# Opening attention on the first 512 rows and running all feed-forward work inside the first 16 attention blocks

## The chip, the core and the metric

The kernel runs on one core of a Trainium2 chip. A core has five engines that run independently and meet through semaphores: TensorE (PE, matmul), VectorE (DVE), ScalarE (ACT), GpSimd (POOL) and SyncE (SP, which here only issues DMAs). Each engine takes its instructions strictly in the order in which the program gave them: an instruction that waits holds up all behind it on that engine. TensorE writes its results to eight PSUM banks of 512 float32 columns; six of them form the ring `ps_r` (three slots of two banks), two are the accumulator `ps_acc` of the attention's values.

The metric is the device time of one execution in microseconds.

## The reference

```
x  = A_x                                  # [1, 2048, 512]
xn = (x - mean(x)) / sqrt(var(x) + 1e-5)  # per row
q  = (xn @ wq) as 32 heads of 128
p  = softmax(q @ k_cache^T / sqrt(128))   # 2048 keys per head
s  = concat_heads(p @ v_cache) @ wo       # back to 512 columns
gate, up = xn @ W_gate, xn @ W_up         # 512 -> 1792
h  = gate * (gate > 0) * up
g  = silu(h @ W_down)                     # 1792 -> 512
out = x + s * g
```

All inputs are bfloat16.

## The kernel before

Rows are taken in four quarters Q of 512. Attention is cut into 128 blocks, one for each head and quarter (head outermost); a block has 8 pairs of 128-key tiles. For a pair, `emit_S_tile` (L1567) computes scores into one ring slot by two matmuls of 512 columns, ScalarE takes their exponential into `PT` (L1579), and `emit_PV_tile` (L1676) multiplies by the values in eight matmuls of 129 columns; the 129th column collects the softmax sum. Scores run three pairs ahead of the values (`LAG`). At the end of a block VectorE takes the reciprocal of the sums and writes the normalised block (`emit_norm_block`, L1596 and L1599), and a DMA on SP turns it (L1604). The value product of the next block waits for that normalisation, since it writes the same banks.

Everything else is placed between these pairs. The main loop (L1964) goes through the pairs in order: scores, then the work that the table `plan` holds for this pair (`emit_M`), then smaller work of `side`, then values. The order on each engine is thus the order in which this loop emits.

Many products are done by seven products in place of eight: two halves of the rows, two halves of the contraction and two halves of the columns are combined by sums beforehand and by VectorE additions afterwards. `emit_st` does so for the query projections of two heads (L914), `emit_gu` for gate and up (L1167), `emit_d` for down (L1228), `emit_unit` and the functions after it for later query and output projections.

What matters around the change:

- Start: x is loaded, normalised and turned; quarter 0 goes through gate, up and down with plain products (`head_ln`, `emit_gate_up(0)`, `emit_down`), before any attention. Then quarter 2 goes through gate and up with plain products (`emit_gate_up(2)`), into whose end the first query projections and scores are woven. Row statistics use VectorE (L419, L424, L436, L439) and a square root on ScalarE (L431); the table of ScalarE's functions is switched from the square root to tanh and exp by an `ACT_TABLE_LOAD`.
- Quarters 1 and 3 go through gate and up as one pair by seven products (`emit_gu`), two products per pair of attention, in pairs 1 to 5 of the blocks 2 to 12. The slab weights come through SP (`gu_load`), are scaled on ScalarE (L626) and combined on POOL (`gu_sums`, L636 to L641).
- Down is done by seven products for quarters 2, 1 and 3 (`emit_d`).
- Query projections of the first eight heads are done by `emit_st`, from weight sums that POOL makes (`emit_sw`, L659 to L672).
- `emit_tx`, `emit_wd_scale`, `emit_wd_sums` and `emit_hs` make the sums that the products by seven need from the rows, the down weights and the hidden values.

From block 16 on nothing of the feed-forward part is left until its result is multiplied in at the end.

Of the kernel before, what the change touches and what calls it, by code (L numbers as in the profile page):

```python
# [5 lines left out]
BF16 = mybir.dt.bfloat16  # L6
# [46 lines left out]
def bass_recurrent_scan__mha_block_cached__glu_gated_reglu__prompt_kernel(  # L53
# [63 lines left out]
    with ExitStack() as es:  # L117
# [9 lines left out]
        def newsem(unit=1):  # L127
# [16 lines left out]
        Wq_sb = [S_([128, DC, 2, Dh], BF16, "Wq_sb") for _ in range(2)]  # L144
        Wo_sb = [S_([128, G, D], BF16, "Wo_sb") for _ in range(2)]
# [4 lines left out]
            "p (i c s) -> p i c s", i=4, c=DC // 2)  # L150
# [8 lines left out]
        o_h, o_wd, o_x = 0, 28672, 43008  # L159
        hT0 = at_(o_h, [128, FC, NQ], BF16, "hT0")  # L160
        hT = [at_(o_h + 14336 * i, [128, FC, NQ], F16, "hT") for i in range(2)]
        Wd_sb = at_(o_wd, [128, FC, D], BF16, "Wd_sb")
        Wd16 = at_(o_wd, [128, FC, D], F16, "Wd16")
        x_sb = at_(o_x, [128, NT, D], BF16, "x_sb")
        WdT = at_(o_x, [128, 3, HF, D // 2], F16, "WdT")
        HS_sb = at_(53760, [128, 3, HF, NQ // 2], F16, "HS_sb")
        xc_sb = at_(59392, [128, 4, D], BF16, "xc_sb")
        xcT = at_(63488, [128, DC, NQ], BF16, "xcT")
        Wg_sb = at_(67584, [128, DC, F], BF16, "Wg_sb")
        Wu_sb = at_(81920, [128, DC, F], BF16, "Wu_sb")  # L170
        gr_sb = [at_(96256 + 1024 * i, [128, NQ], BF16, "gr_sb") for i in range(NSLOT)]
        sig_sb = [at_(99328 + 2048 * i, [128, D], F32, "sig_sb") for i in range(2)]
        small = [103424]

        def sm_(shape, dt, name):
            t = at_(small[0], shape, dt, name)
            small[0] += (4 * shape[1] * (shape[2] if len(shape) > 2 else 1) + 31) // 32 * 32
            assert small[0] <= 104448
            return t

        r2 = sm_([128, 4, 1], F32, "r2")
        r2h = sm_([128, 4, 1], F32, "r2h")
# [4 lines left out]
        nmr = sm_([128, NT, 1], F32, "nmr")  # L187
        rz_sb = sm_([128, 4, 1], F32, "rz_sb")
# [3 lines left out]
        cuv0 = [at_(10240 - 2048 * i, [128, NQ], F32, "cuv0") for i in range(2)]  # L192
        SW0 = at_(12288, [128, 4, DC // 2, Dh], F16, "SW0")
        cuv = [at_(92160 + 2048 * i, [128, NQ], F32, "cuv") for i in range(2)]
        o_w2, o_sg = (64512, 99328, 96256), (104448, 106496, 101376)
# [3 lines left out]
        gcu = [at_(53760 + 2048 * i, [128, NQ], F32, "gcu") for i in range(2)]  # L199
        gcv = at_(57856, [128, NQ], F32, "gcv")  # L200
        uA = [at_(59904 + 1024 * i, [128, NQ], BF16, "uA") for i in range(2)]
        uB = [at_(61952 + 1024 * i, [128, NQ], BF16, "uB") for i in range(2)]
        gA = [at_(o, [128, NQ], BF16, "gA") for o in (66560, 98304)]
        gB = at_(108544, [128, NQ], BF16, "gB")
        dbuf = {Q: [at_(o, [128, 2, D // 2], F32, "dbuf") for o in os_] for Q, os_ in (
            (2, tuple(range(0, 12288, 2048))), (1, o_w2 + o_sg))}
        dbuf[3] = dbuf[1]
# [20 lines left out]
        sem_wg = [newsem(16) for _ in range(4)]  # L228
        sem_wu = [newsem(16) for _ in range(4)]
# [44 lines left out]
        sem_ln3 = newsem()  # L274
        sem_ln4 = newsem()
# [4 lines left out]
        sem_h = newsem()  # L280
        sem_g = newsem()
        sem_qpe = newsem()
        sem_da = newsem()
# [5 lines left out]
        sem_sq = newsem()  # L289
        sem_relu = newsem()  # L290
        sem_sig = newsem()
        sem_exp = newsem()
        sem_tp = newsem()
        sem_gate = newsem()
        sem_gu = newsem()
        sem_y = newsem()
# [17 lines left out]
        FCS = [0, 2, 5, 9, FC]  # L314
        HFC = 2
        wg_src = B_W_gate.rearrange("(c p) f -> p c f", p=128)
        wu_src = B_W_up.rearrange("(c p) f -> p c f", p=128)

        def load_w(eng, dst, src, sems, k):
            a, b_ = FCS[k] * 128, FCS[k + 1] * 128  # L320
            if b_ > a:
                sems[k].sig(eng.dma_start(dst[:, :, a:b_], src[:, :, a:b_]))
# [1753 lines left out]
```

## Time and profile before

| what | value |
|---|---|
| median of 3 runs | 1240.26 us (1240.01 to 1240.39) |
| profiled execution, span from first to last instruction | 1238.8 us |
| instructions in it | 29098 |
| mean granted TensorE clock | 0.999 |

The profile is of one execution, and gives no time of its own for it beside the span; the median of the runs lies 1.5 us above the span. A page of the profile lists the busy time of each engine, then the chain of work that ended last, then groups of instructions by line. A group's row reads: line, engine, operation, tile written <- tiles read, shapes, count | busy time in us, mean ns of one | idle time of the engine before them and what ended it. In the view by stages a row reads: window, length, then the busy time and count of each engine in it, the granted clock, the DMA share and GB/s.

### The profile page before, as it was taken

Reading aid. Unit: us, or ns where it says so; the run is one execution under the profiler, and the core shown is the slowest. Engines: PE = TensorE matmul, PEld = TensorE weight load, DVE = VectorE, ACT = ScalarE, POOL = GpSimd, SP = SyncE. Lnnn points to the kernel's source line nnn. Section 1 sums busy time; section 2 is a strip of 40 time slices with the busy share of each in tenths; the row PEclk is TensorE's granted clock in tenths of the full one; section 3 lists DMA queues with packets and bytes.
Section 4 is the critical chain, followed back from the end, with each engine's and each line's share of the span. In section 5 each row is a group of like instructions: output and inputs, shape, how many; then the busy total and the mean of one; then the engine's idle time right before and its main releaser. Section 6 shows DMA issues by size and latency. Waiting matters only on the chain.

```text
span 1238.8 us, 29098 instructions
## 1 busy us (share of the span) xinstructions
PE 1233.0 (100%) x11937; PEld 817.5 (66%) x11937; DVE 874.2 (71%) x1313; ACT 1040.0 (84%) x1109; POOL 730.2 (59%) x840
## 2 busy tenths in 40 slices
PE   9999999999999999999999999999999999999998
PEld 5466666776666666666666666666666666666665
DVE  7668787667676767676776777676776677675587
ACT  3457877668888998989989999989999989989994
POOL 3355876313757557655866565846775576662368
PEclk9999999999999999999999999999999999999999
DMA  9712331323222333233122332234222322238626
GB/s 276 158 31 37 76 81 24 52 48 96 53 50 52 65 70 52 48 69 60 41 35 52 74 61 51 50 69 69 49 52 50 46 56 48 52 69 129 124 35 141
DMA packets 279012, 85.25 MB, mean 69 GB/s; under 512 B 253024, under 2 KB 278880, under 8 KB 278880
## 3 DMA queue, kind: packets, MB, share of 16 engines
q1 hardware_dynamic: 277536, 82.61, 34.5%
q8 instruction: 95, 1.56, 0.6%
q10 hardware_dynamic: 1344, 0.79, 0.2%
q14 instruction: 37, 0.30, 0.1%
HBM read 36.96 MB, written 4.19 MB: 33 GB/s over the span
## 4 chain that ended last, share of the span: by engine, by line
PE 98%; DVE 1%; DMA 0%; ACT 0%; issue 0%; SPq 0%; DVEq 0%
PE ps_acc L1676 37%; PE ps_r L1567 36%; PE ps_r L1050 5%; PE ps_r L1167 3%; PE ps_r L1406 3%; PE ps_r L1228 3%; PE ps_r L1466 2%; PE ps_r L914 2%; PE ps_r L729 2%; PE ps_r L733 2%; PE ps_acc L832 1%; PE ps_r L1708 1%; PE ps_r L1497 1%; PE ps_r L1498 0%; DMA x_sb<-in_A_x_dram 0%; PE ps_r L1789 0%
## 5 line engine op out<-in xcount | busy, mean ns | idle before, releaser
L1579 ACT ACTIVATE PT<-ps_r 128x1024 bf16<-128x1024 f32 x1024 | 988.6, 1025 | 129.7 <-PE ps_r L1567 117.6
L1676 PEld LDWEIGHTS ps_acc<-V_sb,PT 128*128 128x128 bf16 x8192 | 545.3, 98 | 231.0 <-issue 29.5
L1676 PE MATMUL ps_acc<-V_sb,PT 128*128 128x129 bf16 x8192 | 632.4, 220 | 0.0
L1567 PE MATMUL ps_r<-QT_sb,KT_sb 128*128 128x512 bf16 x2048 | 605.1, 379 | 0.2 <-DVE s_acc L1386 0.2
L1055 DVE TENSOR_TENSOR UVR<-UVR,ps_r 128x512 f32<-128x512 f32 (+1 forms) x228 | 168.6, 755 | 85.3 <-PE ps_r L1050 83.1
L1376 DVE TENSOR_TENSOR s_acc<-s_acc,ps_r 128x1024 f32<-128x1024 f32 x130 | 156.7, 1218 | 32.7 <-PE ps_r L1406 22.5
L1567 PEld LDWEIGHTS ps_r<-QT_sb,KT_sb 128*128 128x128 bf16 x2048 | 161.2, 98 | 26.4 <-DVE UVR L1055 4.3
L1015 POOL TENSOR_TENSOR TI<-xn_sb 128x512 f16<-128x512 f16 x48 | 55.8, 1162 | 97.0 <-PE ps_r L1050 97.0
L1384 DVE TENSOR_TENSOR s_acc<-s_acc,ps_r 128x512 f32<-128x512 f32 x116 | 77.4, 685 | 22.1 <-PE ps_r L1466 17.9
L1599 DVE TENSOR_TENSOR Onorm<-ps_acc,rz_sb 128x512 bf16<-128x512 f32 x127 | 87.8, 691 | 4.4
L1055 DVE TENSOR_TENSOR QT_sb<-UVR,ps_r 128x512 bf16<-128x512 f32 x72 | 49.5, 687 | 52.9 <-PE ps_r L1050 50.5
L1596 DVE RECIPROCAL rz_sb<-ps_acc 128x4 f32<-128x4 f32 x127 | 23.0, 181 | 82.3 <-PE ps_acc L1676 81.7
L1434 POOL TENSOR_TENSOR TI<-OX 128x512 f16<-128x512 f16 x28 | 31.7, 1155 | 65.1 <-issue 65.1
L1015 POOL TENSOR_TENSOR TI<-xnT 128x512 f16<-128x512 bf16 x36 | 41.5, 1154 | 39.7 <-PE ps_r L1050 21.4
L1322 POOL TENSOR_TENSOR WX<-Wo_sb 128x512 f16<-128x512 bf16 x7 | 8.1, 1156 | 90.4 <-DVE Wo_sb L1312 51.3
L1015 POOL TENSOR_TENSOR TI<-xn_sb,TI 128x512 f16<-128x512 f16 x48 | 55.8, 1163 | 0.0
L1123 POOL TENSOR_TENSOR QT_sb<-UVR,UVR 128x512 bf16<-128x512 f32 x24 | 29.8, 1271 | 39.9 <-DVE UVR L1055 39.9
L1050 PE MATMUL ps_r<-TI,SI 128*128 128x512 f16 x126 | 47.8, 379 | 0.0
L1123 POOL TENSOR_TENSOR UVR<-UVR,UVR 128x512 f32<-128x512 f32 x24 | 29.8, 1272 | 25.0 <-DVE UVR L1055 25.0
L1015 POOL TENSOR_TENSOR TI<-xnT,TI 128x512 f16<-128x512 bf16 x36 | 41.6, 1156 | 0.0
L1143 POOL TENSOR_SCALAR gB<-gB 128x512 bf16<-128x512 bf16 x14 | 20.8, 1484 | 30.3 <-DVE gB L1173 30.3
L1434 POOL TENSOR_TENSOR TI<-OT_store 128x512 f16<-128x512 bf16 (+1 forms) x28 | 32.0, 1163 | 9.3 <-issue 8.6
(232 smaller groups left out, 1357.2 us busy)
## 6 DMA issues: line engine op xcount, KB each, us to landing
V_sb<-in_A_v_cache_dram SPq DMA_DIRECT2D x32, 512.0 KB, 4.2
Wq_sb<-in_A_wq_dram SPq DMA_DIRECT2D x16, 256.0 KB, 3.2
Wo_sb<-in_A_wo_dram SPq DMA_DIRECT2D x8, 512.0 KB, 4.6
out_dram<-g_sb SPq DMA_DIRECT2D x4, 512.0 KB, 5.1
OT_store<-Onorm SPq DMA_TRANSPOSE x127, 2.5
Wd_sb<-in_B_W_down_dram SPq DMA_DIRECT2D x1, 1792.0 KB, 14.2
W<-in_B_W_gate_dram SPq DMA_DIRECT2D x14, 128.0 KB, 2.4
W<-in_B_W_up_dram SPq DMA_DIRECT2D x14, 128.0 KB, 3.0
```

The costliest lines, as they stand in the source:

```text
L1015: return sem_ui.sig(pool.tensor_tensor(dst, x, y, o))
L1050: return sem_up.sig(pe.matmul(dst, lhs, rhs, start=start, stop=stop, skip_group_check=True))
L1055: dve.tensor_tensor(dst, x, ps, ALU.add))
L1123: u_tok["add"] = u_tok[("add", i)] = sem_uv.sig(pool.tensor_tensor(dst, UU[:, i, :], RR[:, i, :], ALU.add))
L1167: ins = pe.matmul(ps_r[:, bank, :], L(i), R(i), start=(i == 0), stop=(i == HC - 1))
L1376: t = sem_opa.sig(dve.tensor_tensor(dst, dst, sb, op))
L1384: t = dve.tensor_tensor(dst, dst, sb, op)
L1434: return sem_oi.sig(pool.tensor_tensor(dst, x, y, o))
L1567: ins = pe.matmul(ps_r[:, 2 * s + tt, :], KT_sb[h % 2][:, t * 128:(t + 1) * 128], QT_sb[qt_slot[(h, Q)]][:], start=True, stop=True)
L1579: act.activation(PT[pb][:], ps_r[:, 2 * s:2 * s + 2, :], ACTF.Exp, scale=scale / WSC)
L1599: dve.tensor_tensor(Onorm[ob][:], o_ap, rz_sb[:].to_broadcast([128, 4, Dh]), ALU.mult))
L1676: ins = pe.matmul(o_ap, PT[pb][:, tt, j * 128:(j + 1) * 128], V_sb[vb][:, t, 0:VW], start=(t == 0 and j % 2 == 0), stop=(t == KT - 1 and j ...
```

## The change

Order of the work. The first 512 rows are normalised, turned on TensorE, and at once projected to the queries of heads 0 to 3 by plain products (`front`). Attention opens then. The blocks of heads 0 and 1 alternate for the first eight blocks (`hq_of`), so that the quarters 1 to 3 are needed later; their queries for heads 0 and 1, and quarter 2 for heads 2 and 3, come from plain products in the loop (`emit_qplain`). The other rows' coefficients use a reciprocal square root by Newton steps on VectorE in place of ScalarE's square root.

```diff
+        def front():
+            c0 = head_first_transpose(head_norm(0))
+            warm_mm(3)
+            nt = {n: head_norm(n) for n in range(1, 4)}
+            act.activation(warm_sb[:], eps_sb[:], ACTF.Tanh)
+            slots = [ring_acquire() for _ in range(HQ // 2)]
...
+            _wait(pe, c0[0])
+            head_q(0, al, range(0, DC // 2))
+            _wait(pe, c0[1])
+            head_q(0, al, range(DC // 2, DC))
+            c1 = head_transpose(1, nt[1])
+            _wait(pe, c1)
+            head_q(1, lo, cc)
+            c2 = head_transpose(2, nt[2])
+            head_q(1, hi, cc)
+            c3 = head_transpose(3, nt[3])
+            _wait(pe, c2)
+            head_q(2, al, cc)
+            _wait(pe, c3)
+            p = head_q(3, al, cc)
+            toks = {0: q_out(act, 0, 0, ps_r[:, 0, :], p[0])}
+            stok = [ln_stats(4), ln_stats(5)][-1]
+            toks[1] = q_out(dve, 1, 0, ps_r[:, 1, :], p[1])
+            ring_tok[0] = [toks[0], toks[1]]
+            stok = [ln_stats(6), ln_stats(7)][-1]
+            for h in (2, 3):
+                toks[h] = q_out(dve, h, 0, ps_r[:, h, :], p[h])
+            ring_tok[1] = [toks[2], toks[3]]
+            ctok = ln_coef(list(range(4, 8)), stok)
+            ln_rows_norm(1, ctok)
+            ln_rows_turn(1)
+            for Q in (2, 3):
+                ctok = ln_rows(Q)
+                if Q == 3:
+                    gu_prep(0, pool)
+                ln_rows_norm(Q, ctok)
+                if Q == 2:
+                    ln_rows_turn(2)
+            gu_prep(1, pool)
...
+            op(dve.tensor_scalar(v, mv[:, a:b_, 1:2], 1e-5, None, op0=ALU.add))
+            op(dve.tensor_scalar(t.bitcast(I32), v.bitcast(I32), 1, None, op0=ALU.logical_shift_right))
+            tok = op(dve.tensor_scalar(y.bitcast(I32), t.bitcast(I32), -1.0, float(0x5f3759df), op0=ALU.mult, op1=ALU.add))
+            for _i in range(3):
+                op(dve.tensor_tensor(t, y, y, ALU.mult))
+                op(dve.scalar_tensor_tensor(t, t, -0.5, v, op0=ALU.mult, op1=ALU.mult))
+                tok = op(dve.scalar_tensor_tensor(y, t, 1.5, y, op0=ALU.add, op1=ALU.mult))
...
+        def hq_of(b):
+            if b < 2 * QB:
+                return b % 2, b // 2
+            return divmod(b, QB)
```

Here `head_norm` normalises one row tile (coefficients, then the scaling on VectorE for tile 0 and on POOL for the others), `head_q` gives the short query matmuls of a row tile, and `op` waits for its own result before the next.

Feed-forward. All four quarters go through gate and up by seven products, as the row pairs (0, 2) and (1, 3): 28 slabs, two products in each pair of attention, in a cycle of seven steps for two slabs. One ring slot is held for the whole of it, and the products of a slab are added up in its banks: a product may start when the bank's last partial sum has been read. Down follows by seven products for all four quarters, in the order 2, 0, 3, 1.

```diff
+        gu_cycle = (((0, 1, 0), (0, 6, 1)), ((0, 2, 0), (0, 5, 1)), ((0, 3, 1), (0, 7, 0)),
+                    ((1, 1, 1), (0, 4, 0)), ((1, 2, 1), (1, 6, 0)), ((1, 5, 0), (1, 7, 1)),
+                    ((1, 3, 0), (1, 4, 1)))
+        gu_steps = [[(c + o, m, k) for o, m, k in st] for c in range(0, NCH, 2) for st in gu_cycle]
...
+            if m == 1:
+                _wait_all(pe, [t[(c, "s")], t.get((c - 1, "gB"))])
+                if k == 0:
+                    _wait_all(pe, xt_ready[pair] + xt_ready[pair + QB // 2])
+            elif m == 6:
+                _wait_all(pe, [t[(c, "x")], t.get((c - 1, "uA"))])
+                if k == 0:
+                    _wait(pe, tx_tok[(pair, 3)])
+            else:
+                _wait(pe, t[(c, {2: "c1", 5: "c6", 3: "c65", 7: "gA", 4: "uB"}[m])])
...
+        def gu_hi(c):
+            pair, k = divmod(c, FC)
+            _wait_all(dve, [gu_tok[(c, "gB")], gu_tok[(c, "uB")]])
+            if pair and k == 0:
+                _wait(dve, (sem_dp, 7))
+            h_done[(pair + QB // 2, k)] = sem_gud.sig(
+                dve.scalar_tensor_tensor(hT[1][:, k, :], gB[:], 0.0, uB[:], op0=ALU.max, op1=ALU.mult))
...
+        def emit_gu(n):
+            if not gu_slot:
+                gu_slot.append(ring_acquire(hold=True))
+            s = gu_slot[0]
+            st = gu_steps[n]
+            for c, m, k in st:
+                p = gu_prod(c, m, 2 * s + k)
+                gu_out(c, m, 2 * s + k, p)
+                if m == 3:
+                    hi_c = c
+            if any(m == 3 for _, m, _k in st):
+                gu_hi(hi_c)
+            for c, m, k in st:
+                if m == 4 and c + NW < NCH:
+                    gu_load(c + NW)
+                    gu_later.append((n + 4, c + NW))
+            if gu_later and n >= gu_later[0][0]:
+                gu_prep(gu_later.pop(0)[1])
```

`gu_out` reads a partial sum: product 2 by ScalarE (ReLU), the others by VectorE; after product 4 POOL multiplies the lower quarter's hidden values, and `gu_hi` does the upper quarter's on VectorE. `gu_prep` scales a slab on ScalarE and makes its four sums on POOL (slabs 0 and 1 on POOL alone).

The places, in pairs P counted from the first (block P // 8, pair P % 8):

```diff
+        GU0, GU1 = 13, 67
...
+        for n in range(len(gu_steps)):
+            half = len(gu_steps) // 2
+            put(GU0 + n if n < half else GU1 + n - half, (emit_gu, 0, n))
+        for P, h, Q in ((8, 0, 1), (10, 1, 1), (20, 0, 2), (24, 1, 2), (30, 0, 3), (34, 1, 3), (38, 2, 2), (42, 3, 2)):
+            put(P, (emit_qplain, 1, h, Q))
+        for P, pr, c, step in ((46, 1, 1, 0), (50, 1, 1, 1), (54, 1, 1, 2), (61, 1, 1, 3),
+                               (76, 2, 0, 0), (82, 2, 0, 1), (88, 2, 0, 2), (94, 2, 0, 3),
+                               (98, 2, 1, 0), (104, 2, 1, 1), (108, 2, 1, 2), (113, 2, 1, 3)):
+            put(P, (emit_st, 1 if step == 3 else 2, pr, c, step))
+        for Q, ps in ((2, (63, 64, 65, 66)), (0, (68, 69, 70, 71)),
+                      (3, (117, 118, 119, 120)), (1, (122, 123, 124, 125))):
+            for k, P in enumerate(ps):
+                put(P, (emit_d, 1 if k == 3 else 2, Q, k))
+        for Q, ps in ((2, (53, 54, 55, 56, 62, 62, 62, 63)), (0, (66, 66, 67, 67, 67, 68, 68, 68)),
+                      (3, (106, 107, 108, 109, 115, 116, 116, 117)), (1, (120, 120, 120, 121, 121, 121, 122, 122))):
+            for k, P in enumerate(ps):
+                aside(P, emit_hs, Q, k // 4, k % 4)
+        aside(8, ln_rows_turn, 3)
+        for k in range(4):
+            aside(10 + k // 2, emit_tx, 0, k)
+            aside(17 + k, emit_tx, 1, k)
+            aside(30 + 6 * k, emit_wd_sums, k)
+        aside(20, load_wd)
+        aside(25, emit_wd_scale, 0)
+        aside(28, emit_wd_scale, 1)
+        aside(36, lambda: (_wait(sp, qp_done_tok[0]), issue_wq(2)))
+        aside(43, emit_sw, 1)
+        aside(68, emit_sw, 2)
...
+            if (bq, pq) == (12, 4):
+                emit_sw(3)
```

The loads of keys, values and query weights of the first heads move to the very start, on SP and ACT; the keys of head 2 are loaded at the start of block 7, one block ahead.

781 lines of the change are left out of this document (277 added, 504 removed).

## The prediction

> **What bounds the kernel now.** I read the page first: the span, the busy shares and the chain that ended last.
>
> ```profile
> span 1238.8 us, 29098 instructions
> PE 1233.0 (100%) x11937; PEld 817.5 (66%) x11937; DVE 874.2 (71%) x1313; ACT 1040.0 (84%) x1109; POOL 730.2 (59%) x840
> PE 98%; DVE 1%; DMA 0%; ACT 0%; issue 0%; SPq 0%; DVEq 0%
> ```
>
> The page warns that a matmul's end is modelled, so I also took the view of who waited for whom, for PE (us, times, longest). First and last of its four rows:
>
> ```profile
> PE ps_r L475 <- PEq L2061: 0.8, 1, 0.8
> ...
> PE ps_r L1567 <- DVE s_acc L1386: 0.2, 1, 0.2
> ```
>
> The largest is 0.8 us, and that lies before the first matmul: TensorE waits next to nothing in the whole span. It is the bound everywhere, so the change pays by matmul time that it takes away, and costs by every microsecond for which TensorE has nothing it may start. That ScalarE's exponentials begin earlier is worth nothing. True paces come from the chain in order of time (start, us, what):
>
> ```profile
> 9.08 1.79 PE ps_r L541 x32
> 31.59 12.09 PE ps_acc L832 x56
> 74.51 3.06 PE ps_r L1228 x28
> 312.94 0.91 PE ps_acc L1676 x16
> ```
>
> A matmul costs 0.056 us at 128 columns, 0.216 at 512, 0.109 at 256, and 0.057 in the attention's value product. One pair of attention is 2 x 0.216 + 8 x 0.057 = 0.89 us.
>
> **Matmul work.** Stage view, whole span, restricted in turn to lines 729, 733, 832, 1167, 914 and 1228; count in brackets:
>
> ```profile
> 0.00:1238.80 1238.80, 26.69 (x104) 10.06 (x104) 1.00 0.35 69
> 0.00:1238.80 1238.80, 26.69 (x104) 10.17 (x104) 1.00 0.35 69
> 0.00:1238.80 1238.80, 12.25 (x56) 5.49 (x56) 1.00 0.35 69
> 0.00:1238.80 1238.80, 50.46 (x196) 19.13 (x196) 1.00 0.35 69
> 0.00:1238.80 1238.80, 29.42 (x112) 10.78 (x112) 1.00 0.35 69
> 0.00:1238.80 1238.80, 34.08 (x294) 28.52 (x294) 1.00 0.35 69
> ```
>
> Of 512 columns 208 + 56 + 196 + 112 = 572 go. They are replaced by 28 slabs x 7 products x 2 = 392 for gate and up, 8 x 4 = 32 in emit_qplain, and 14 + 28 + 28 = 70 in emit_st: 494. Down grows from 294 to 4 x 98 = 392 of 256 columns. The 64 short gate/up matmuls of the head become 64 short query matmuls. Net: -78 x 0.216 + 98 x 0.109 = **-6.1 us**. From the seventeenth block on, the instructions are those of before: 0.
>
> **The front.** Rows of the timeline (start, us):
>
> ```profile
> 3.49 0.69 DVE L419 BATCH_NORM_STATS2 stats<-x_sb 128x6 f32<-128x512 bf16 x1 [3.49 <-DMA x_sb<-in_A_x_dram]
> 9.12 0.58 ACT L467 COPY xcT<-ps_acc 128x512 bf16<-128x512 bf16 x1 [0.62 <-PE ps_acc L462]
> 10.70 1.03 PE L729 MATMUL ps_acc<-xcT,Wg_sb 128*128 128x512 bf16 x4
> 14.53 0.16 DVE L436 RECIPROCAL rstd<-sqv 128x4 f32<-128x4 f32 x1
> 14.72 0.16 DVE L439 SCALAR_TENSOR_TENSOR nmr<-mv,rstd 128x4 f32<-128x4 f32 x1
> 16.52 0.38 DVE L424 BATCH_NORM_AGGREGATE mv<-stats 128x2 f32<-128x6 f32 x4
> 31.37 1.28 ACT L840 ACT_TABLE_LOAD   x1
> 206.19 0.69 DVE L1173 TENSOR_TENSOR gcu<-gcu,ps_r 128x512 f32<-128x512 f32 x1 [0.21 <-PE ps_r L1167]
> 206.79 0.68 DVE L1173 TENSOR_TENSOR uB<-gcv,ps_r 128x512 bf16<-128x512 f32 x1
> ```
>
> By 10.70 us the old kernel has run 80 short matmuls (4.5 us): 6.2 us lost, then nothing. In the new one a row tile costs VectorE statistics 0.69, aggregate 0.2, a root on ScalarE 0.2 with two hand-overs, reciprocal 0.16: about 1.35 us, so the fourth root ends near 9.2. ScalarE then loads the tanh table (1.28), and the copies of tiles 1 to 3 are queued behind it: the first ends near 11.3. Copies, transposes and 48 short matmuls alternate until about 14.5; the first scores start near 14.7. VectorE takes three head outputs and two statistics from 14.2 to 17.3 (0.6 us from one operation to the next), then three coefficient chains: 4 aggregates 0.38 and 12 dependent small operations at 0.19, 2.8 us; the second and third with 4 statistics, 5.3 us each. It is free at **30.7**. The first block's normalisation is queued behind them (0.9 us), and the ninth value product waits for that: 31.6. TensorE, in order, has by then run 80 short matmuls, 12 score pairs, 8 value pairs and one emit_qplain: 4.5 + 5.2 + 3.6 + 0.9 = 14.2 us. Lost 17.4 against 6.2: +11.2. Then four emit_tx (0.6 to 0.69 each) stand between VectorE's next query output and the first slab's product 6: +0.9. **Front +12.1.** Bounds: if the dependent small operations ran at the aggregates' 0.1, 36 x 0.09 = 3.3 less; and never under 14.7 - 4.5 - 6.2 = +4.0, the first score's own delay.
>
> [...]
>
> ```profile
> 0.76 3.92 PE L475 MATMUL ps_r<-const-bfloat16-1.0 128*128 128x256 bf16 x18 [0.76 <-PEq L2061]
> ```
>
> Those 18 run at 0.22 us where 256 columns cost 0.109 later, so a slow start is seen; a fall back is not, TensorE never idling so long. [...]
>
> **Queues and loads.**
>
> ```profile
> KT_sb<-in_A_k_cache_dram SPq DMA_TRANSPOSE x32, 4.2
> W<-in_B_W_up_dram SPq DMA_DIRECT2D x14, 128.0 KB, 3.0
> L1579 ACT ACTIVATE PT<-ps_r 128x1024 bf16<-128x1024 f32 x1024 | 988.6, 1025 | 129.7 <-PE ps_r L1567 117.6
> L626 ACT ACTIVATE W<-W 128x1024 bf16<-128x1024 bf16 x14 | 14.7, 1052 | 1.4 <-DMA W<-in_B_W_up_dram 1.4
> ```
>
> The third head's keys, moved on SP to one block ahead, have 8 pairs (14 us) for 4.2. A slab has four pairs (7 us) for 3.0 plus issue; SP has issued its loads by the time the rows 4 to 15 are there to be turned, and the block's own transposes stand behind those turns; nothing of it is asked for before VectorE's 30.7. ScalarE per pair: 1.03, and per seven pairs two 0.6 copies and two scales: 1.5 of 1.75 us. I cost these at 0; without the cover a late slab holds ScalarE, and the exponentials with it, by its lateness.
>
> **The gate/up stretch** (98 pairs). A pair becomes 0.43 scores, 0.86 two products, 0.46 values: 1.75 us. Products now add up in a bank, so each waits on PE for VectorE's (twice in seven pairs ScalarE's) reading of the one before; scores and values stand behind it. From the pair's start, first product done 0.86, VectorE 0.2 later (row of the 0.69 read above: after its product, 0.2), done 1.75, needed 2.18; second read done 2.4, needed 2.61. Little over 0.2 us is spare.
>
> ```profile
> L1599 DVE TENSOR_TENSOR Onorm<-ps_acc,rz_sb 128x512 bf16<-128x512 f32 x127 | 87.8, 691 | 4.4
> L1596 DVE RECIPROCAL rz_sb<-ps_acc 128x4 f32<-128x4 f32 x127 | 23.0, 181 | 82.3 <-PE ps_acc L1676 81.7
> L1250 DVE SCALAR_TENSOR_TENSOR g_sb<-dbuf,dbuf 128x512 bf16<-128x512 f32 x12 | 10.1, 848 | 0.3
> L768 DVE TENSOR_SCALAR Wd_sb<-Wd_sb 128x3584 bf16<-128x3584 bf16 x2 | 2.8, 1416 | 0.0
> ```
>
> *Block ends.* Old plans leave pairs 6 and 7 of a block without products; now VectorE's normalisation (0.18 + 0.69) queues behind this pair's reads and the next value product needs it at 3.04. After two reads it ends at 3.4 (0.4 late), after one 0.15 late, after three (gu_hi, not in the trace, 0.69 to the 0.85 of the nearest row; I take 0.7) 1.0 late. Of twelve ends in the stretch four, three and five are of three, one and two reads: 4.0 + 0.45 + 2.0 = **+6.5**.
>
> *Bursts.* Single extra operations (emit_tx, a query output) fit the room or come with their own matmuls. Around pairs 53 to 56 and 106 to 109, though, three pairs bring VectorE 13 operations at 0.64 (8.3 us; the first also a normalisation) against 3 x 1.75 + 0.86 = 6.1 of TensorE: about 2 us late each. emit_wd_scale (1.4) twice, less the room: 0.5 each. **+5.** Both terms lie between 0 (reads overlap more) and twice that (VectorE holds 0.9 of the stretch, one lateness feeding the next).
>
> *POOL.*
>
> ```profile
> L659 POOL TENSOR_SCALAR Wq_sb<-Wq_sb 128x1024 bf16<-128x1024 bf16 x2 | 5.5, 2774 | 6.4 <-DMA Wq_sb<-in_A_wq_dram 6.4
> L636 POOL TENSOR_TENSOR SG<-W 128x256 f16<-128x256 bf16 x14 | 9.3, 667 | 17.4 <-ACT PT L1579 13.3 <-ACT W L626 4.1
> L445 POOL TENSOR_SCALAR xn_sb<-x_sb,rstd,nmr 128x512 bf16<-128x512 bf16 x16 | 12.1, 768 | 21.1 <-DVE nmr L439 21.1
> L1145 POOL TENSOR_TENSOR hT<-gA,uA 128x512 f16<-128x512 bf16 x14 | 16.5, 1180 | 1.2 <-DVE uA L1173 1.1
> L779 POOL TENSOR_TENSOR WdT<-Wd_sb 128x1792 f16<-128x1792 bf16 x1 | 3.6, 3569 | 0.0
> ```
>
> In the front POOL normalises rows 4 to 7 from 20.1, rows 8 to 11 from 25.4 (3.1 us each), then gu_prep(0), 2.8 + 4 x 0.67 = 5.5, until 34.0, rows 12 to 15 until 37.1 and gu_prep(1) until 42.6; product 6 of the two slabs asks at about 36.5 and 45: 0, but 1 to 2 us if the front comes out 2 to 3 us shorter. The crowded place is later. From pair 41: scale 2.6 us, sums 2.7, emit_wd_sums 3.6, emit_sw(1) 2.8 + 2.7, one h 1.2, next sums 2.7: 18.2 us, needed by pair 48 at 7 x 1.75 + 2 x 0.86 + 0.86 = 14.8. **+3.3**, from 0 (earlier stalls give POOL time) to 6 (another 2.7 of backlog).
>
> **Sum.** In the profiled execution: 1238.8 - 6.1 + 12.1 + 6.5 + 5 + 3.3 = 1259.6 us of span. The span lies 1.5 us under the median of the runs, 1240.26: **1261 us**.
>
> **Rivals.**
> 1. *VectorE keeps pace in the stretch*, only the front and a little POOL is paid: 1240.3 - 6.1 + 12.1 + 1 = 1247. For it: the old stretch runs with VectorE at 79% of the time without a stall,
>
> ```profile
> 97.00:220.00 123.00, 123.00 (x1058) 75.92 (x1056) 97.72 (x162) 94.02 (x101) 84.23 (x93) 1.00 0.29 56
> ```
>
> (DVE 97.72 of 123). Against: there a product never waited for the reading of the last. Chance 0.22.
> 2. *Not slower*: VectorE is done with the row coefficients before the ninth value product needs it, so the front costs only its floor, +4.0, and the stretch runs free: 1240.3 - 6.1 + 4.0 = 1238; without the table load ahead of the copies 1.5 less. It decides at about 25 us, where the eighth exponential is done; VectorE free by then makes this case. Against: 36 dependent operations at 0.19. Chance 0.12.
> 3. *Lateness feeds itself*: with one bank pair held, VectorE's and POOL's lateness add instead of hiding each other, 0.2 us more in each of 98 pairs: 1281. Chance 0.10.
> 4. *The array slows again*: TensorE's idle stretch from about 7.2 to 11.3 us is followed by 48 matmuls at twice 0.056: +2.7, 1264. Chance 0.06. [...]
>
> **Chances.** Forecast 0.50. Runs of this kernel differ by 0.4 us; 0.2% (2.5 us) is about what a measurement tells from no change. Case 2 straddles that line: faster 0.06, same 0.06; all others are slower: 0.88. The range leaves out case 2 and the upper half of case 3: 1243 to 1280.
>
> **What would show it.** PE's waits should name VectorE in the first 32 us and the value product there; VectorE should be solid from about 14 to 31; between about 36 and 240 us PE's gaps should sit at block ends (VectorE Onorm), near pairs 54 to 56 and 108 to 110 (VectorE), and once near pair 48 (POOL sums); after block 16 the pace should be that of before. Few gaps in the stretch make case 1; the first scores well before 14 us, or VectorE free near 25, would break the front's sum.

## The result and the profile after

The change makes the kernel slower: 1302.2 us (1300.3 to 1303.0) against 1240.26, a ratio of 1.0498 (95%: 1.0483 to 1.0513). That is +62 us where the prediction said +21, and outside its range. The direction was right; the size forecast was a third of what came.

The page of the kernel after, its first lines and the granted clock in 40 slices:

```profile
span 1301.6 us, 29330 instructions
PE 1250.4 (96%) x11957; PEld 819.3 (63%) x11957; DVE 929.2 (71%) x1389; ACT 1049.4 (81%) x1114; POOL 778.6 (60%) x879
PEclk8899999999999999999999999999999999999999
```

TensorE, which had nothing to wait for before, is now idle for 1301.6 - 1250.4 = 51.2 us (before: 5.8). The stage view of the kernel after tells where (stretch, its length, busy us of PE, PEld, DVE, ACT and POOL with counts, granted clock, DMA share, GB/s):

```profile
0.00:34.50 34.50, 22.91 (x194) 15.95 (x195) 22.57 (x79) 18.17 (x26) 19.87 (x19) 0.87 0.84 179
34.50:67.00 32.50, 23.90 (x164) 13.18 (x165) 17.55 (x25) 14.68 (x16) 29.67 (x22) 0.88 0.27 54
67.00:160.00 93.00, 80.34 (x563) 41.09 (x560) 75.48 (x107) 53.18 (x60) 63.09 (x63) 0.96 0.31 70
160.00:216.00 56.00, 50.61 (x429) 34.56 (x428) 44.57 (x67) 28.75 (x35) 21.00 (x24) 1.00 0.22 43
216.00:268.00 52.00, 50.38 (x376) 26.74 (x376) 41.22 (x67) 35.99 (x40) 28.18 (x36) 1.00 0.35 70
268.00:345.00 77.00, 70.17 (x607) 47.40 (x605) 60.90 (x92) 41.43 (x49) 31.36 (x32) 0.98 0.18 42
345.00:1301.60 956.60, 952.10 (x9638) 640.33 (x9636) 666.87 (x956) 857.21 (x892) 585.48 (x686) 1.00 0.34 64
```

Length less PE's busy time gives 11.6, 8.6, 12.7, 5.4, 1.6, 6.8 and 4.5 us idle. From 345 us on the kernel is as fast as before, as forecast: from the first value product of pair 136 to the end, both timelines have 954.5 us. The granted clock is a second loss: 0.13 of the first stretch, 0.12 of the second, 0.04 of the third and 0.02 of the sixth are 13.6 us at most, since some of the low clock falls into idle time. With 6.1 us of matmul work less, some 10 of the 62.8 us between the spans are in neither loss. A part of them lies in the modelled ends: a score matmul is shown 0.38 us long (381 ns mean) where the next follows after 0.216, so every gap hides some 0.16 us of itself in the instruction before it, by estimate 7 us for the 44 waits of the whole view. The rest was not traced.

Who was waited for, PE's waits of the kernel after (us, times, longest):

```profile
PE ps_r L1037 <- DVE c L1051: 6.9, 7, 1.9
PE ps_r L758 <- DMA xnT<-xn_sb: 5.4, 1, 5.4
PE ps_r L1037 <- POOL SG L617: 5.4, 2, 3.4
PE ps_r L1037 <- POOL W L607: 5.2, 2, 4.4
PE ps_acc L1590 <- DVE Onorm L1513: 3.4, 3, 1.4
PE ps_r L1481 <- ACT PT L1493: 3.0, 2, 1.5
PE ps_r L1481 <- DVE QT_sb L792: 2.8, 4, 1.0
PE ps_r L1481 <- DVE cuv L792: 2.2, 2, 2.0
```

The forecast had one wait on POOL (3.3 us near pair 48; it came, 2.0 us before the product at 132.8 us) and block ends on Onorm as the main row of the stretch. Instead three things stand there that it did not have: POOL late by 10.6 us, the turned rows late by 5.4, and single waits of 1.6 to 2.0 us on VectorE's c and cuv. Four groups of the kernel after begin to explain them (busy us and mean ns):

```profile
L431 POOL TENSOR_SCALAR xn_sb<-x_sb,mv,rstd 128x512 bf16<-128x512 bf16 x15 | 30.9, 2072 | 13.9 <-DVE rstd L425 8.8 <-DVE rstd L409 5.1
L615 POOL TENSOR_TENSOR SG<-SG,W 128x256 f16<-128x256 f16 x28 | 20.9, 747 | 0.0
L1081 DVE SCALAR_TENSOR_TENSOR hT<-gB,uB 128x512 f16<-128x512 bf16 x28 | 27.5, 982 | 0.5
L1159 DVE SCALAR_TENSOR_TENSOR g_sb<-dbuf,dbuf 128x512 bf16<-128x512 f32 x16 | 15.1, 966 | 0.0
```

A row's normalisation on POOL takes 2.07 us in its new form (subtract, then multiply), 0.77 in the old (multiply, then add). And gu_hi, costed at 0.7 us, takes 0.98 in the mean. The timelines show why. POOL's, around 100 to 140 us (start, us):

```profile
100.93 3.58 POOL L670 TENSOR_TENSOR WdT<-Wd_sb,WdT 128x1792 f16<-128x1792 bf16 x1
...
119.09 3.58 POOL L672 TENSOR_TENSOR Wd<-Wd_sb 128x1792 f16<-128x1792 bf16 x1
...
136.48 3.58 POOL L674 TENSOR_TENSOR WdT<-WdT,Wd_sb 128x1792 f16<-128x1792 f16 x1
```

and VectorE's in the same time:

```profile
102.13 2.94 DVE L1081 SCALAR_TENSOR_TENSOR hT<-gB,uB 128x512 f16<-128x512 bf16 x1
114.29 0.69 DVE L1081 SCALAR_TENSOR_TENSOR hT<-gB,uB 128x512 f16<-128x512 bf16 x1
120.57 2.64 DVE L1081 SCALAR_TENSOR_TENSOR hT<-gB,uB 128x512 f16<-128x512 bf16 x1
...
137.94 2.67 DVE L1081 SCALAR_TENSOR_TENSOR hT<-gB,uB 128x512 f16<-128x512 bf16 x1
```

The sums end at 104.51, 122.67 and 140.06; the three gu_hi beside them at 105.07, 123.21 and 140.61, each some 0.55 us later, whenever it began. It is not slowed but held until POOL is done. VectorE's readings of the matrix banks (L1052, 0.67 to 0.69 us in all 140) are never longer. Nor does every POOL operation hold gu_hi to its end. POOL's rows, then VectorE, around 50 us:

```profile
45.11 8.25 POOL L431 TENSOR_SCALAR xn_sb<-x_sb,mv,rstd 128x512 bf16<-128x512 bf16 x4
51.87 0.72 DVE L1081 SCALAR_TENSOR_TENSOR hT<-gB,uB 128x512 f16<-128x512 bf16 x1
```

The last of these four rows runs from 51.3 to 53.4 us, and gu_hi is done at 52.6. At 268.86 it takes 0.69 us inside a POOL scaling of 2.77. In the traces of the new order it ended eleven times before the TENSOR_SCALAR of POOL (one tensor input) beside which it ran (in the kernel after 0.76 us before the end of the row at 51.29, and 0.06 before that of the scaling); the POOL operations that held it were all TENSOR_TENSOR (two).

**Theory** after this: the missing 41 us are POOL's row form, VectorE held up beside POOL, and matmuls at half rate behind the gaps. **Rival**: VectorE simply has too much to do in the stretch, so that one lateness feeds the next and these places are only where it shows.

### The profile page after: what moved, and what is told of

Same layout as the page of the kernel before. It is cut to its first block, busy times and chain, and to the rows that moved or that the text cites. A ratio compares the mean times of both kernels' runs of the same rounds, so it can differ in the third digit from the quotient of the medians.

```text
span 1301.6 us, 29330 instructions
## 1 busy us (share of the span) xinstructions
PE 1250.4 (96%) x11957; PEld 819.3 (63%) x11957; DVE 929.2 (71%) x1389; ACT 1049.4 (81%) x1114; POOL 778.6 (60%) x879
## 4 chain that ended last, share of the span: by engine, by line
PE 80%; DVE 3%; issue 1%; ACT 0%; DVEq 0%; ACTq 0%
PE ps_acc L1590 33%; PE ps_r L1481 31%; PE ps_r L920 5%; PE ps_r L1320 3%; PE ps_r L1380 2%; PE ps_r L1037 2%; PE ps_r L1129 2%; PE ps_r L1622 1%; PE ps_r L787 1%; DVE g_sb L1159 1%; PE ps_r L1411 1%; PE ps_r L1412 0%; DVE uB L1052 0%; ACT PT L1493 0%; PE ps_r L1703 0%
## 5 line engine op out<-in xcount | busy, mean ns | idle before, releaser
L1073 POOL TENSOR_TENSOR hT<-gA,uA 128x512 f16<-128x512 bf16 x28 | 36.3, 1298 | 77.7 <-DVE uA L1052 51.7
L1052 DVE TENSOR_TENSOR c<-c,ps_r 128x512 f32<-128x512 f32 x56 | 38.5, 687 | 28.1 <-PE ps_r L1037 26.5
L1037 PE MATMUL ps_r<-xn_sb,SG 128*128 128x512 f16 x168 | 49.6, 391 | 6.7 <-POOL SG L617 5.4
L1037 PE MATMUL ps_r<-xnT,W 128*128 128x512 bf16 x112 | 34.7, 393 | 13.5 <-DVE c L1051 6.9
```

Of the source, the lines that this page charges most:

```text
L1037: ins = pe.matmul(ps_r[:, bank, :], L(i), R(i), start=(i == 0 and m in (1, 6, 7)), stop=(i == HC - 1 and m in (2, 3, 4)), skip_group_check ...
L1052: dve.tensor_tensor(dst[:], a[:], ps, ALU.add))
```

## The experiments

Times are medians, with the ratio to the kernel before and its 95% interval. The four runs of one kernel spread by 0.8 to 4.4 us, so a difference between two rows is good to some 2 us (an estimate from these spreads).

| run | us | ratio |
|---|---|---|
| after | 1302.2 | 1.0483 to 1.0513 |
| e1_row_form | 1293.5 | 1.0413 to 1.0444 |
| e3_row_form_two_steps | 1290.3 | 1.0392 to 1.0427 |
| e2_sums_split | 1296.4 | 1.0438 to 1.0469 |
| e4_hi_on_pool | 1311.6 | 1.0557 to 1.0588 |
| e5_sums_early | 1287.4 | 1.0370 to 1.0401 |
| e6_table_late | 1290.8 | 1.0394 to 1.0429 |
| e7_pool_thin | 1276.2 | 1.0277 to 1.0308 |
| e8_no_hi | 1275.5 | 1.0267 to 1.0298 |
| e9_hi_one_input | 1284.4 | 1.0338 to 1.0369 |
| e10_thin_no_hi | 1267.5 | 1.0203 to 1.0233 |
| e11_sums_earlier | 1285.8 | 1.0352 to 1.0387 |
| e12_warm | 1291.7 | 1.0394 to 1.0425 |
| e13_hi_as_stats | 1282.7 | 1.0324 to 1.0355 |
| e14_extra_stats | 1310.8 | 1.0544 to 1.0580 |
| e15_all_mended | 1283.5 | 1.0328 to 1.0359 |

e1, e2 and e4 start from the kernel after; e3 is e1 with one edit more; e5 to e15 start from e3.

### The rows on POOL, and the chains behind them

```diff
-                eng.tensor_scalar(xrow(n), x_sb[:, n, :], mv[:, n, 0:1], rstd[:, n, 0:1],
-                                  op0=ALU.subtract, op1=ALU.mult))
+                eng.tensor_scalar(xrow(n), x_sb[:, n, :], rstd[:, n, 0:1], nmr[:, n, 0:1],
+                                  op0=ALU.mult, op1=ALU.add))
```

with nmr, minus mean times rstd, from one more scalar_tensor_tensor per chain.

> The sixteen row normalisations take their old form again (x times rstd plus nmr, with one small VectorE operation per chain for nmr). Theory (POOL's row operation in the new form, 2.07 us for the 0.77 that was forecast, is most of what the first blocks lose): the row falls to about 0.77 us; TensorE's waits on the turned rows (5.4 us), on the scaled slab (5.2) and on the slab's sums at 41 us (3.4) go, but VectorE's row chains still end at about 33.5 us, so the wait for them takes the place of the 5.4; what is won is 5.2 + 3.4 and some 3 us of half-rate matmuls behind these gaps: 1289 to 1293 us. Rival (lateness of the adding products feeds itself, whatever begins it): other waits take the place, 1298 to 1302 us.

Measured 1293.5, 8.7 us less than after. The row and the waits of e1 (group of POOL; then PE's waits):

```profile
L438 POOL TENSOR_SCALAR xn_sb<-x_sb,rstd,nmr 128x512 bf16<-128x512 bf16 x15 | 11.3, 768 | 21.6 <-DVE nmr L404 21.6
```

```profile
PE ps_acc L1597 <- DVE Onorm L1520: 9.4, 6, 4.8
...
PE ps_r L765 <- DMA xnT<-xn_sb: 2.2, 1, 2.2
PE ps_r L1044 <- POOL SG L624: 1.9, 1, 1.9
```

The row is back at 0.77 us, and the wait on the scaled slab (5.2) and the early one on its sums (3.4) are gone: 8.6 us, about what was won. The wait for the turned rows falls from 5.4 to 2.2, but a wait of 4.8 for VectorE's first Onorm stands right behind it, and the ninth value product starts at 36.2 us for 34.5 in the kernel after: in the front the slow rows had hidden the slow chains, and what was won lies behind it. So the first part of the theory holds.

e3 takes one of three Newton steps out of each chain, 9 small operations:

```diff
-            for _i in range(3):
+            for _i in range(2):
```

> As the run before, and two Newton steps instead of three in each of the three coefficient chains: 9 small VectorE operations of about 0.2 us fewer, 1.8 us. Theory (once POOL's rows are quick, VectorE's chains set the end of the front): 1.5 to 1.8 us less than with the old row form alone. Rival (the turned rows or the first scores set it): no difference between the two, under 0.5 us.

Measured 1290.3, 3.1 us less than e1, more than the 1.8 us of the operations; e1 ran between 1292.1 and 1294.2 and e3 between 1289.8 and 1293.1, so the surplus says nothing. The ninth value product starts at 34.25 us for 36.17 in e1, 1.9 earlier: once the rows are quick, VectorE's chains set the end of the front, as the prediction had it.

### VectorE beside POOL's sums

```diff
-                t = pool.tensor_tensor(WdT[:, 1], b22, WdT[:, 0], ALU.subtract)
...
+            for i in range(HF):
+                t = sem_wdt.sig(pool.tensor_tensor(dst[:, i, :], a[:, i, :], b[:, i, :], ALU.subtract))
```

> Each of the four sums of the down weights on POOL, one operation of 1792 columns (3.58 us), becomes seven of 256; the rest as after. Theory (a VectorE operation whose two inputs both lie in SBUF, begun beside a POOL operation, ends only some 0.55 us behind the end of that one): gu_hi beside the sums falls from 2.6 to 2.9 us to at most 1.4; the three TensorE waits of 1.9, 1.6 and 2.0 us behind them fall to under 1.5 us together; 1296 to 1299 us, POOL's four sums growing from 14.3 to about 19 us. Rival (both engines share a rate): gu_hi is stretched by the same amount in all, the waits stay, 1301 to 1304 us.

Measured 1296.4, 5.8 us less. VectorE's timeline of e2, the three gu_hi that run beside pieces of these sums alone:

```profile
95.13 1.22 DVE L1076 SCALAR_TENSOR_TENSOR hT<-gB,uB 128x512 f16<-128x512 bf16 x1
116.59 0.69 DVE L1076 SCALAR_TENSOR_TENSOR hT<-gB,uB 128x512 f16<-128x512 bf16 x1
134.52 1.02 DVE L1076 SCALAR_TENSOR_TENSOR hT<-gB,uB 128x512 f16<-128x512 bf16 x1
```

In pieces POOL's sums hold VectorE for one piece only, though each sum now takes longer (seven pieces, 4.9 us for 3.58); no gu_hi of e2 takes over 1.22. That is the hold, and no sharing of a rate. In that time none of TensorE's waits on c and cuv is over 0.8 us (1.9, 1.6 and 2.0 in the kernel after), but POOL itself is later by a little: 2.8 us on SG for 2.0, and 1.5 on Wq_sb.

```diff
-                dve.scalar_tensor_tensor(hT[1][:, k, :], gB[:], 0.0, uB[:], op0=ALU.max, op1=ALU.mult))
+            r = sem_hp.sig(pool.tensor_scalar(gB[:], gB[:], 0.0, None, op0=ALU.max))
...
+                pool.tensor_tensor(hT[1][:, k, :], gB[:], uB[:], ALU.mult))
```

> gu_hi goes from VectorE to POOL as two operations (max with 0, then the product); the rest as after. VectorE loses 28 operations of 0.98 us mean, 27.5 us; POOL gains about 28 x 2.6 = 73 us. Theory (in the stretch TensorE waits for VectorE's readings, which stand behind gu_hi): the waits on c, gB, uB, cuv, QT_sb and Onorm fall to less than half, 1290 to 1296 us, unless POOL's sums then come late. Rival (the waits come from the chain product, reading, product itself and not from VectorE's load): unchanged waits, 1300 to 1304 us.

Measured 1311.6, 9.4 us more than after. The waits on VectorE's c (L1051) did fall from 6.9 to 1.4 us, but those on gB rose from 1.3 to 5.3, since VectorE now waits for POOL before it writes gB and uB again, and POOL took the place of the others, as PE's waits of e4 show:

```profile
PE ps_r L1037 <- POOL SG L617: 8.0, 5, 2.9
...
PE ps_r L787 <- POOL Wq_sb L635: 5.2, 1, 5.2
...
PE ps_r L1131 <- POOL hT L1083: 3.2, 1, 3.2
```

POOL has no room for it either.

The sums were then put elsewhere, in three pieces each:

```diff
-            aside(30 + 6 * k, emit_wd_sums, k)
+            aside((29, 33, 37, 41)[k], emit_wd_sums, k)
```

> The run with the old row form and two Newton steps (1290.3 us), and on top of it the four sums of the down weights in three pieces each and five to seven pairs earlier or so (behind pairs 29, 33, 37, 41 instead of 30, 36, 42, 48). Theory (VectorE held up beside POOL's long sums, and POOL's backlog near pair 48): the waits of 1.9, 1.6 and 0.4 us behind gu_hi and that of 1.9 us on the slab's sums go: 1283 to 1286 us. Rival (POOL is now crowded earlier instead, the same time is lost there): 1289 us or more.

Measured 1287.4: 2.9 us less than e3, not 4 to 7. The long waits behind gu_hi went (the longest on c is 1.2 us for 1.9), but POOL's backlog near pair 47 grew: one wait of 2.8 us on SG for 1.9. Putting them at pairs 23 to 34, with the load and the scaling earlier too:

```diff
-        aside(20, load_wd)
+        aside(16, load_wd)
...
-            aside(30 + 6 * k, emit_wd_sums, k)
+            aside((23, 27, 30, 34)[k], emit_wd_sums, k)
```

> On top of the 1290.3 us kernel: the down weights are loaded at pair 16 and scaled at 20 and 22, and their four sums, in three pieces each, stand behind pairs 23, 27, 30 and 34, so that POOL has none of them from pair 36 on. All of the result is computed. Theory (the run with them at 29 to 41 lost 3.4 us near pair 47 to POOL's backlog in place of the waits that it removed): SG's wait near pair 47 under 0.5 us, no gu_hi over 2.2 us, 1281 to 1284 us. Rival (POOL's load in the stretch as such): the wait appears earlier, 1286 us or more.

Measured 1285.8, again short of the theory's range: the wait on SG falls to 1.1 us, and one of 1.8 us on c appears at 60 us instead. Both places are full; moving POOL's work moves the waits and wins part.

### Hold or load?

```diff
-            a11, a12 = W[:, 0:HC, 0, :], W[:, HC:DC, 0, :]
+            a11, a12 = W[:, 0:HC, 0, 0:16], W[:, HC:DC, 0, 0:16]
...
-            aside(30 + 6 * k, emit_wd_sums, k)
```

> On top of the same 1290.3 us kernel: POOL's sums of the gate/up slabs are made on 16 of 128 columns, and the sums of the down weights are left out (the products read other weights in their place); so a part of the result isn't computed. TensorE's, VectorE's and ScalarE's instructions stay. Between pairs 20 and 132 that kernel loses some 35 us. Theory (VectorE is held up beside POOL, and POOL is late itself): 12 to 20 us of them go, 1270 to 1278 us, gu_hi at 0.7 us. Rival (VectorE's own load and the adding products cause them): 2 to 6 us go, 1284 to 1288 us.

Measured 1276.2, 14.1 us less than e3, within the theory's range. gu_hi with little beside it, from e7's groups:

```profile
L1092 DVE SCALAR_TENSOR_TENSOR hT<-gB,uB 128x512 f16<-128x512 bf16 x28 | 19.6, 699 | 0.5
```

```diff
-        H = hT[Q // 2]
+        H = hT[0]
...
-                dve.scalar_tensor_tensor(hT[1][:, k, :], gB[:], 0.0, uB[:], op0=ALU.max, op1=ALU.mult))
```

> On top of the same 1290.3 us kernel: gu_hi is left out, and the down products of the upper rows read the lower rows' h; so a part of the result isn't computed. VectorE has 28 operations of 0.98 us fewer, 0.69 of it its own time and 0.29 time spent held up beside POOL. Theory (held up beside POOL): about what the run with thin POOL wins, 8 to 14 us, and not more than that run: 1276 to 1282 us. Rival (VectorE's own load): clearly more than the run with thin POOL, 15 us or more, under 1275 us.

Measured 1275.5, 14.9 us less: more than the theory allowed, less than the rival asked. Both edits in one kernel:

> The run with thin POOL (1276.2 us) and that without gu_hi (1275.5) in one; a part of the result isn't computed. Each won 14 to 15 us alone. Theory (most of what gu_hi costs is that it is held up beside POOL, so the two win the same microseconds): 1266 to 1272 us. Rival (VectorE's load and POOL are separate causes): the sum of both, 1260 to 1262 us.

Measured 1267.5: 22.9 us less than e3, where the two sum to 29.0. A part is common and a part is not; the theory's range held, but it doesn't decide.

```diff
-                dve.scalar_tensor_tensor(hT[1][:, k, :], gB[:], 0.0, uB[:], op0=ALU.max, op1=ALU.mult))
+                dve.tensor_scalar(hT[1][:, k, :], c_65[:], 0.0, 1.0, op0=ALU.max, op1=ALU.mult))
```

> On top of the 1290.3 us kernel (old row form, two Newton steps): gu_hi stays one VectorE operation of 512 columns, but with one SBUF input (the maximum of c_65 and 0, in place of the product of gB's maximum and uB); so a part of the result isn't computed. VectorE's number of operations stays, POOL's work too. Theory (an operation with two SBUF inputs is held until the POOL operation beside it is done, one with a single input is not): no operation of this line over 0.75 us, the waits of 1.9 and 1.6 us on c go, 1283 to 1286 us. Rival (POOL slows everything that VectorE does beside it): the line still has operations of over 2 us, 1288 to 1291 us.

Measured 1284.4, and the reason given was wrong. VectorE's timeline of e9:

```profile
76.86 0.43 DVE L1088 TENSOR_SCALAR hT<-c 128x512 f16<-128x512 f32 x1
84.50 1.72 DVE L1088 TENSOR_SCALAR hT<-c 128x512 f16<-128x512 f32 x1
...
91.03 2.66 DVE L1088 TENSOR_SCALAR hT<-c 128x512 f16<-128x512 f32 x1
```

An operation with one SBUF input is held as well: that at 91.03 ends at 93.69, 0.30 us behind POOL's sum, which runs from 89.82 for 3.57. It is shorter alone (0.43), so both hold and load fell, and the run tells nothing between them.

So a VectorE operation was sought that isn't held. The row statistics in the front of the kernel after ran beside POOL's rows, four in 2.47 us (which alone proves little, since POOL's rows did not hold gu_hi to their end either):

```profile
21.67 2.47 DVE L398 BATCH_NORM_STATS2 stats<-x_sb 128x6 f32<-128x512 bf16 x4
```

```diff
-                dve.scalar_tensor_tensor(hT[1][:, k, :], gB[:], 0.0, uB[:], op0=ALU.max, op1=ALU.mult))
+            sem_gud.sig(dve.bn_stats(dump[:, 0, :], gB[:]))
```

> As the run without gu_hi (1275.5 us), with one row statistics operation on gB in gu_hi's place: 0.69 us each in the front, and there not longer beside POOL's rows. So VectorE's load is that of the 1290.3 us kernel, without the hold; a part of the result isn't computed. Theory (what gu_hi costs is the hold beside POOL): no such operation over 0.75 us, 1275 to 1280 us. Rival (what gu_hi costs is its own 0.69 us on a full VectorE): 1285 to 1290 us.

In e14 the same line is added and gu_hi kept.

> The 1290.3 us kernel with one such statistics operation more ahead of each gu_hi, 28 x 0.69 = 19 us of VectorE's time; all of the result is computed. Theory (VectorE has room, only the holds hurt): 1291 to 1294 us. Rival (VectorE is full): 8 us or more, 1298 us and up.

e13: 1282.7, between the two. The groups of e13 and of e14:

```profile
L1086 DVE BATCH_NORM_STATS2 dump<-gB 128x6 f32<-128x512 bf16 x28 | 19.2, 686 | 0.0
```

```profile
L1090 DVE SCALAR_TENSOR_TENSOR hT<-gB,uB 128x512 f16<-128x512 bf16 x28 | 31.0, 1106 | 0.0
L1086 DVE BATCH_NORM_STATS2 dump<-gB 128x6 f32<-128x512 bf16 x28 | 19.3, 690 | 0.5
```

Now the statistics run beside the four long sums too, and none takes over 0.69 us. Same load, no hold: 7.6 us of the 14.9 that gu_hi costs are the hold (1290.3 to 1282.7), 7.2 its own 19.2 us of VectorE (1282.7 to 1275.5). The hold goes both ways and e13 lifts both: POOL's products of hidden values, which take up to 1.61 us in e3, take 1.16 at most in e13. The four runs of e13 lie between 1281.7 and 1285.2, so the two shares are rough, but neither is small: both are right in part. e14 took 1310.8, 20.4 us more than e3, far past the rival's 8: 19.3 us of statistics, and gu_hi held 5.2 us longer (31.0 against 25.8 in e3), 24.5 us of VectorE in all, of which a share of 0.83 comes out at the end. VectorE is full in this stretch: what is added costs nearly its whole length, what is taken away (0.37 per us in e8 against e13) wins less and less.

### The start, and what all of it gives

The line that loads the tanh table moves:

```diff
-            act.activation(warm_sb[:], eps_sb[:], ACTF.Tanh)
             slots = [ring_acquire() for _ in range(HQ // 2)]
...
+            act.activation(warm_sb[:], eps_sb[:], ACTF.Tanh)
             _wait(pe, c2)
```

> On top of the same 1290.3 us kernel, the tanh table's load (1.28 us on ScalarE) goes behind the copies of the second and third row tile instead of ahead of them. Theory (the load holds the copies, the copies the first scores, and these VectorE's chains): TensorE's wait on the copy of 1.5 us goes and everything behind it comes 1.0 to 1.6 us earlier: 1288.7 to 1289.3 us. Rival (the front's end hangs on the loads of rows 4 to 15): no change, 1290 us.

Measured 1290.8, as e3 (1290.3), although the first scores come at 16.7 us for 17.5.

```diff
+            warm_mm(14)
             for k in range(2):
                 _wait(pe, wq_tok(k))
...
+            warm_mm(12)
             _wait(pe, c1)
```

> On top of the 1290.3 us kernel: 14 and 12 further matmuls of 256 columns on constants, into a bank nobody uses yet, where TensorE waits for the first query weights and for the copy of the second row tile. All of the result is computed. Theory (short matmuls after these two gaps run at half rate, 0.107 instead of 0.056 us): the query matmuls of the first four row tiles take 0.056 us throughout, the first scores come 1.5 to 2.5 us earlier and the time falls by as much, 1288 to 1289 us. Rival (the gaps are there anyway, and the rate behind them is hidden by the copies): first scores and time as without, 1290 us.

Measured 1291.7, no gain. TensorE's timeline of e3, then of e12:

```profile
14.35 3.27 PE L510 MATMUL ps_r<-xnT,Wq_sb 128*128 128x128 bf16 x32
17.46 1.13 PE L1488 MATMUL ps_r<-QT_sb,KT_sb 128*128 128x512 bf16 x4
...
96.64 0.61 PE L1044 MATMUL ps_r<-xnT,W 128*128 128x512 bf16 x2 [1.87 <-DVE c L1058]
```

```profile
13.48 1.96 PE L510 MATMUL ps_r<-xnT,Wq_sb 128*128 128x128 bf16 x32
15.46 1.04 PE L1490 MATMUL ps_r<-QT_sb,KT_sb 128*128 128x512 bf16 x4
...
94.68 0.60 PE L1046 MATMUL ps_r<-xnT,W 128*128 128x512 bf16 x2 [1.88 <-DVE c L1060]
```

The mechanism is right: kept busy, TensorE runs the 32 short matmuls in 1.96 us for 3.27, the first scores come 2.0 us earlier, and at the wait on c near 95 us it is still 1.96 us ahead. There it loses the lead. The wait is the same in both, 1.9 us, but in e12 half rate follows it, in e3 not; the stage view of e12, then of e3, behind that wait:

```profile
96.00:100.00 4.00, 4.00 (x18) 2.02 (x17) 1.54 (x3) 0.59 (x1) 3.05 (x5) 0.60 0.00 0
```

```profile
98.00:102.00 4.00, 4.00 (x32) 2.17 (x30) 3.06 (x6) 1.57 (x2) 3.02 (x5) 1.00 0.00 0
```

So neither the theory nor the rival: the start's gain is real and not hidden, but another half-rate stretch of 0.4 x 4 = 1.6 us took it back in the profiled execution: the value product of pair 40 starts at 102.29 us in e12 and at 102.58 in e3, 0.3 ahead for 2.0.

The edits of e1, e3, e11, e6 and e12 together, with 6 matmuls for 12 in the second gap:

> All that was found, together, with the full result: old row form, two Newton steps, down weights' sums in three pieces at pairs 23 to 34, the tanh table behind the copies, 14 and 6 further matmuls in the first gaps. Theory (the parts add up: 1285.8 for the sums, 1 to 2 us for the start): 1281 to 1285 us. Rival (what the start wins is lost again at the next wait): 1285 to 1287 us. Either way over 1240: the order itself costs more than its 6.1 us of matmul time.

Measured 1283.5: the theory's range, 2.3 us under e11. With the full result this is the best version of the new order, 18.7 us under the kernel after and 3.4% (3.3 to 3.6) over the kernel before. None of the runs beats the kernel before, those that leave work out included.

## Why the prediction was wrong

- **Matmul work, -6.1 us: right.** The counts are those forecast (392 of L1037 among 512 columns), and behind 345 us the kernel is that of before.
- **Front, +12.1: nearly right in size, by another cause.** The ninth value product was to go on at 31.6 us and did at 34.5, 2.9 later. The first scores came at 16.3 us for 14.7, VectorE's chains ended at 33.4 for 30.7. What TensorE waited for, though, were the turned rows, made late by POOL; only e1 uncovered the chains behind them.
- **"POOL normalises rows 4 to 7 ..., 3.1 us each": the first step that failed.** 0.768 us was the row of the old form; the new one takes 2.07. Fifteen rows bring 19.6 us more on POOL, and the ledger that put both slabs' sums at cost 0 broke: 8.7 us (e1).
- **"gu_hi ..., not in the trace, 0.69 to the 0.85": the second.** It takes 0.69 alone and up to 2.94 beside POOL's sums, 27.5 us in all for the 19.6 of the forecast; the hold costs some 7.6 us of the time (e13 against e3), and splitting the four sums alone won 5.8 (e2). The trace of before did show 848 ns in the mean for g_sb, of the same kind with two SBUF inputs; its twelve take from 0.68 to 1.64 us, so it had sometimes been held. I read the mean as an upper bound.
- **"Little over 0.2 us is spare": right, and that is why it mattered.** e14 shows that there is no room in the stretch: a lengthening of VectorE comes out by 0.83. The terms of +6.5 for block ends and +5 for bursts were sums of single places, as if lateness at one went away before the next. Block ends were fewer (2.1 us in two waits on Onorm, the third, 1.4, lying behind the stretch), the bursts came where named, but the pairs with emit_d (waits of 2.8 us at 166 to 206 and 1.8 at 303 to 335) had been costed at nothing.
- **POOL near pair 48, +3.3: right in place and within its bounds** (2.0 us).
- **Rivals.** The third (lateness feeds itself, 1281 us, 0.10) was the nearest, though the losses do not lie in each of 98 pairs: the first fifteen rows of the view of waits, 38 waits, hold 43.9 of the 51.2 idle us. The fourth (half rate, 0.06; that an idle stretch brings it I assumed, the trace of before does not show it) came as described and was too small: the clock stood at 0.50 from 8.25 to 15.08 us, with PE busy for 5.57 of them, so some 2.8 us for its 2.7; but six more stretches of 3.4 us at 0.50 came between 32 and 292 us, behind gaps that the forecast did not have. Behind the 5.4 us gap of the kernel after, four matmuls of 512 columns take 1.87 us, where the next four take 1.03:

```profile
32.56 1.87 PE L758 MATMUL ps_r<-xnT,Wq_sb 128*128 128x512 bf16 x4 [5.41 <-DMA xnT<-xn_sb]
36.75 1.03 PE L758 MATMUL ps_r<-xnT,Wq_sb 128*128 128x512 bf16 x4
```

Of the 41 us between forecast and time, 8.7 are shown to be the row form. POOL in the stretch (hold and late sums) costs 14.1 by e7, of which the forecast had 3.3. What the other 21 or 22 are is not shown: the front was 2.9 us later than forecast, and VectorE's fullness, the half rate and the pairs with emit_d are left; how they share the rest was not measured. With the rows mended, POOL thin and gu_hi left out, e10 stands at 1267.5, still 6 us over the forecast.

## What to carry to other kernels

Cost an operation by its own form: the same tile as (subtract, multiply) cost 2.7 times what it cost as (multiply, add) on POOL here. Before SBUF work is put on VectorE and POOL at once, list which VectorE operations read and write SBUF alone: each (the row statistics of e13 excepted) may have to wait for the longest two-input POOL operation beside it, 3.58 us here (gu_hi took up to 2.94), so such POOL operations are split or put where VectorE only reads the matrix banks. And where a queue has a tenth of its time to spare, sum its lateness along the stretch and not place by place; an experiment that adds a known load tells how full it is.

## What the runs showed of the hardware that was not expected

- A hold has no size of its own: gu_hi ended 0.55 us behind POOL's operation three times, with 2.94, 2.64 and 2.67 us in all. The row statistics (0.69 us, also beside sums of 3.58) and every reading of the matrix banks (0.67 to 0.69 us in all 140 of L1052) were not held, and POOL operations with one tensor input (rows of 2.07 us, scalings of 2.77) did not hold gu_hi to their end.
- POOL suffers too: the slab's sums, 0.67 us in the mean in the kernel before (L636) and where no VectorE operation on SBUF alone is beside them, take 0.71 to 0.75 in the mean after.
- The half rate comes back after gaps of 1.9 us, and not after each: the same gap brought it in e12 and not in e3, whose work before it lay 2 us later. In the traces of the new order the changes of the granted clock lie on a grid of 3.41 us (in the kernel after all fifteen, from 8.25 us to 1301.90). In e12 the gap (92.80 to 94.68 us) falls whole into one step of it, 92.37 to 95.79, and the next step has 0.50; in e3 (94.76 to 96.64) it is cut at 95.62 (eight steps ahead of the half rate from 122.9 to 126.3), and both steps are followed by 1.00. Over the first 360 us of the sixteen traces of the new order, a step at full clock with less than 1.8 us of TensorE's idle time (its waits as the profile has them) was never followed by one at half (1507 steps), with more than 2.15 us always (34), and in between 21 of 34 times. In the kernel after alone, seven steps at full clock were followed by one at half, with 1.88 us or more of idle time each, and the 90 others have 1.73 or less.
- The new order's times spread by 0.8 to 4.4 us from run to run, those of the kernel before by 0.3 to 1.6. The granted clock goes with it (e13: 0.997 at 1281.7 us, 0.991 at 1285.2), so the half rate may be why, which wasn't tried.
